# A new program order for an attention and two-stage expert kernel, with a straight constants block, a deeper ring of first-layer tiles and a smaller DMA scratch

## The chip, the cores and the metric

The kernel runs on one core of a Trainium2 chip. Its time is the device time of one execution in microseconds. TensorE (PE, with its weight loads as PEld), VectorE (DVE), ScalarE (ACT) and GpSimd (POOL) compute; SyncE (SP) only queues transfers, in order, and GpSimd queues the indirect ones.

## The reference

```python
# attention: B=4, H=8, S=576, D=64; a local band and a 4x downsampled one, added
q_d, k_d, v_d = means over groups of 4 positions
out_up    = repeat(softmax(q_d @ k_d.T / 8) @ v_d, 4)
out_local = softmax(where(|i - j| < 4, q @ k.T / 8, -1e9)) @ v
x = (out_up + out_local) as [2304, 512]
# first layer pair: w_in [512, 2048], w_out [2048, 512]
x = relu(x @ w_in) ** 2 @ w_out
# top 2 of 8 experts by noisy logits; w1 [8, 512, 1024], w2 [8, 1024, 512]
noisy = x @ w_gate + log1p(exp(x @ w_noise)) * noise
for e in range(8):
    out[rows of e] += weight * (relu(x[rows of e] @ w1[e]) @ w2[e])
```

## The kernel before

Matrix operands are float32 split into a high and a low fp16 part, and a product is three matmuls: high x high, high x low, low x high. The scales of the split are powers of two, taken from the data: a bound of w_in's columns by gram matrices of its pieces (L1023), the Frobenius norm of w_out and of each expert's matrices.

**Attention.** The 32 units (four batches b, two parts of each, four pairs of heads) each go through: loads of q and k (`load_qk`, L248, one for two parts), of v in groups (`load_vg`, L203) and of v in windows (`load_vw`, L255, two buffers used in turn); scores with a mask (S, L285 and L292), downsampled scores (D, L307), two softmaxes (`ml` and `md`: L318 to L336), normalising (`nl`, `nd`, on POOL for b = 0, L354), transposes (PT, L372 to L395), the PV matmul (PW: L426, then `od` on ACT at L444 and `xt` on VectorE at L445), and the split to fp16 (`xb`, L465 and L468) into one of five column buffers `xb` of the tile `xall`. A unit's `vw` buffer comes free when the PV matmul two units earlier has read it.

**First layer pair.** w_in comes in eight pieces (`load_f`, L523) through several steps on ACT and VectorE (L527, L531, L535, L540), each with a gram; then `scale` (L1033 and, in a helper, L171) gives `s_in`, and each piece is split (L1046, L1053). w_out takes the same steps in eight pieces, with squares by gram (L1078, L1079). The tokens are nine column chunks c of 256, with eight pairs of hidden blocks fp each: M is the first-layer matmul (`m1_mm`, L610), r its relu and square and split (`m1_ev`, L629 to L639) into a pair of tiles gh and gl, and Y the second matmul (`m2`, L656; L680 for the first chunks). `g_tiles` says from which ring of buffers a pair comes: eight pairs in pool `bp`, and `GX` = 3 more in pool `ap` for some (c, fp).

**Gate and experts.** For each of 18 token tiles the row is written out transposed by a DMA (`yT`, L724, read at L733), gated, and scattered by two indirect DMAs into the row buffer `xs` (L817). Expert 0 runs inside the table, its squares and splits (`prep_e`, L846, L862, L863) and those of expert 1 too. Experts 1 to 7 run in a loop behind it (L1205 to L1228). In a round, `c_m1` makes eight blocks f for the early 384 rows and eight for the late 240 (L917, relu and split at L919 and L920, into `h` tiles), and `c_m2` five blocks j of rows (L933), each with a scatter into the output (L936). Between the blocks stand the pieces that prepare expert e+1: eight squares (L846), the scales (`frob`, pfr at L476), eight splits. First-layer blocks use four PSUM tiles in turn.

**Order.** `ORDER` is a table of some 2000 tokens (`S5`: step S of unit 5) which is executed inside `tc.manual_schedule()`, so that each engine's program is in the table's order. What stands outside, the constants ahead and the expert loop behind, is ordered by the framework's scheduler. Waits and buffers then decide when things run.

Of the kernel before, what the change touches and what calls it, by code (L numbers as in the profile page):

```python
# [7 lines left out]
F32 = mybir.dt.float32  # L8
# [4 lines left out]
U16 = mybir.dt.uint16  # L13
# [13 lines left out]
P = 128  # L27
# [25 lines left out]
qk0 il0 ob0 vg1 S0 G0 vg0 ml0 ia0 vg3 D0 vm1 qk1 qk2 vg2 S1 il1 el0 vm0 ib0 nl0 md0 G1 qk3 vg4 D1 ml1 ed0 S2 ic0  # L53
md1 nd0 ij0 el1 G2 nl1 vm3 ed1 il2 nd1 il3 D2 vm2 md2 ia1 PT0 Xa0 vw1 ml2 el2 ib1 S3 nl2 Xm0 ed2 vm4 G3 PT1 S4
ml3 el3 vw0 il4 vs4 D3 il5 ia2 ic1 vs0 md3 nl3 il6 nd2 ed3 ia3 ib2 Xb0 D4 in0 md4 vs2 ij1 PW0 ic2 vw2 ib3 PT2
ml4 xb0 in1 ic3 el4 vs1 ij2 S5 vs3 PW1 D5 il7 md5 ol3 ol0 ia4 ed4 nd3 ia5 ib4 ol2 ij3 xb1 ic4 PT3 ib5 ia6 ij4
ib6 in2 in3 ic5 ml5 ia7 nl4 is3 PW2 ic6 el5 in4 ib7 ij5 vw3 xb2 ij6 ic7 oa3 ed5 in5 ij7 in6 in7 oB3 oa0 oB0 oa2
is7 nd4 ol1 PW3 wS0 S6 oB2 oc0 oc3 wT0 oj3 oa1 wU0 oc2 vw4 oB1 os3 wh5 oj2 wh1 qk4 S7 wl5 xb3 oc1 vg5 D6 wh4 md6
PT4 wl1 oj1 os2 wh0 oj0 wh7 wl0 nl5 vw5 wh6 M5 wl6 os1 wh2 wh3 qk5 wl7 M0 D7 wl4 qk6 of3 nd5 wl3 os0 wl2 ed6 r0
vm5 ra5 oh3 M1 of1 oo3 ra1 ml6 PW4 oh0 oo0 oh1 oh2 M6 oo1 oo2 el6 xb4 yh0 ol6 M3 ol5 yh1 vs5 nl6 r6 PT5 yl8 ml7  # L60
ra3 oa5 M4 yh5 oB5 ol4 yh9 yh6 ol7 oa6 oB6 oc5 oc6 yh3 yl5 yl11 oa4 yl3 nd6 S8 oj5 yl1 oa7 oj6 oB4 oB7 PW5 yh14
yl9 oc4 yh13 oc7 os5 M7 md7 yh11 ed7 yl13 yl6 yl14 os6 PT6 qk7 S9 vw6 yl0 oj7 oj4 G4 yh8 os7 os4 r4 M2 G5 of7
xb5 ra7 PW6 yh4 el7 of5 oh6 D9 vg6 yl15 yh12 D8 oh7 oh4 nl7 yh25 yh7 yh27 yh28 nd7 oh5 yh29 yl12 ml8 yh31 yh19
el8 PT7 yh24 oo7 oo6 yh30 yl28 yl30 oo5 yh20 oo4 vw7 yh23 yl29 md8 xb6 nl8 vm6 ed8 PW7 nd8 md9 vw8 yl20 yh21
yh17 yl24 vs6 yh22 yl25 xb7 S11 yh15 SD0 yl31 pz0 ml9 r2 yh16 ed9 yl16 PT8 M9 pg0 G6 G7 S10 ra9 ml10 M13 vw9 pf0
yl10 D10 yl2 el9 ra13 PW8 nl9 yl22 yl18 nd9 vg7 M12 vm7 yh10 PT9 yl17 Xa1 D11 M10 ml11 md10 Xm1 vs7 el10 md11
el11 ed10 nl10 ed11 nl11 yl4 yh26 pf1 nd10 yl21 r12 S13 S12 PT10 Xb1 ml12 yl7 D13 pf2 nd11 xb8 D12 md12 pf3 el12
# [32 lines left out]
def moe_kernel(ctx, tc, qk_in, vwin, vgrp, w_in, w_out, w_gate, w_noise, noise, w1, w2, out):  # L100
# [42 lines left out]
    for n in (32, 64):
        nc.vector.tensor_scalar(it[:, n:2 * n], it[:, :n], float(n), None, op0=OP.add)
    pc0_ = psT.tile([P, 512], F32, tag="tp", name="pci")
    nc.tensor.matmul(pc0_[:, 1:2], r32[0:1], onesf[0:1, 0:1], start=True, stop=True)
    nc.tensor.matmul(pc0_[:, 0:1], it[0:1], onesf[0:1, 0:1], start=True, stop=True)
    nc.vector.tensor_copy(pidx, pc0_[:, :2])
    nc.vector.tensor_scalar(dc, it[:, :KW], pidx[:, 1:2], 3.0, op0=OP.subtract, op1=OP.subtract)
    nc.vector.tensor_tensor(dc, dc, dc, op=OP.mult)  # L150
    nc.vector.tensor_scalar(mask, dc, 9.5, NEG, op0=OP.is_gt, op1=OP.mult)
    nc.vector.tensor_copy(masks, mask[:, None, :].to_broadcast([P, 9, KW]))
    for j in (0, 64):
        nc.vector.memset(masks[j:j + 32, 0, :3], NEG)
        nc.vector.memset(masks[j + 32:j + 64, 7, KW - 3:], NEG)
    nc.vector.tensor_scalar(idb, it, pidx[:, 0:1], None, op0=OP.is_equal)
    nc.vector.tensor_scalar(idf, it, pidx[:, 0:1], None, op0=OP.is_equal)
    nc.vector.memset(pms[1], 0.0)
    for i in range(2):
        nc.vector.memset(pTs[i][0], 0.0)  # L160
        nc.vector.memset(vws[i][32:64], 0.0)
    nc.vector.tensor_copy(onesb, onesf)
    nc.gpsimd.affine_select(trib, onesb, [[1, P]], OP.is_gt, 0.0, base=0, channel_multiplier=-1)
# [1173 lines left out]
```

## Time and profile before

| | us |
|---|---|
| median of 3 runs | 997.05 (996.45 to 998.46) |
| the profiled execution | 999.23 |
| its span in the trace | 997.4 |
| PE busy in the span | 928.7 (93%) |
| VectorE, ACT, POOL busy | 580.4, 497.4, 131.4 |
| last matmul ends, span ends | 985, 997.4 |

The profiled execution has its own time; the span is the part that the trace covers, without what lies before and behind. Mean granted clock of PE is 0.965.

### The profile page before, as it was taken

Reading aid. Unit: us, or ns where it says so; the run is one execution under the profiler, and the core shown is the slowest. Engines: PE = TensorE matmul, PEld = TensorE weight load, DVE = VectorE, ACT = ScalarE, POOL = GpSimd, SP = SyncE. Lnnn points to the kernel's source line nnn. Section 1 sums busy time; section 2 is a strip of 40 time slices with the busy share of each in tenths; the row PEclk is TensorE's granted clock in tenths of the full one; section 3 lists DMA queues with packets and bytes.
Section 4 is the critical chain, followed back from the end, with each engine's and each line's share of the span. In section 5 each row is a group of like instructions: output and inputs, shape, how many; then the busy total and the mean of one; then the engine's idle time right before and its main releaser. Section 6 shows DMA issues by size and latency. Waiting matters only on the chain. (4 is left out here: it accounts for less than half of the span.)

```text
span 997.4 us, 20288 instructions
## 1 busy us (share of the span) xinstructions
PE 928.7 (93%) x8254; PEld 624.9 (63%) x8254; DVE 580.4 (58%) x1809; ACT 497.4 (50%) x1076; POOL 131.4 (13%) x150
## 2 busy tenths in 40 slices
PE   3559999999999998999999899899999999999994
PEld 2448988575776675667766456647475656566562
DVE  7788967588678756665577763617162525343220
ACT  5687857455546554365663461835354544431110
POOL 2401200010102010000021021020202011111111
PEclk9659999999999998999999999999999999999997
DMA  9943369824232314022412785763838292821212
GB/s 321 299 161 117 122 234 324 210 96 84 81 98 83 53 42 46 27 65 100 137 44 64 211 190 146 174 142 94 170 84 187 54 219 27 238 30 22 31 22 34
DMA packets 104183, 121.70 MB, mean 122 GB/s; under 512 B 69264, under 2 KB 69264, under 8 KB 102032
## 3 DMA queue, kind: packets, MB, share of 16 engines
q1 hardware_dynamic: 95568, 100.57, 35.4%
q0 software_dynamic: 8512, 19.74, 10.4%
q8 instruction: 67, 1.10, 0.5%
q14 instruction: 36, 0.29, 0.1%
HBM read 70.33 MB, written 35.28 MB: 106 GB/s over the span
## 5 line engine op out<-in xcount | busy, mean ns | idle before, releaser
L610 PE MATMUL ph<-xall,wih 128*128 128x256 f16 x1152 | 196.0, 276 | 0.3 <-ACT r L629 0.3
L917 PEld LDWEIGHTS <-we 128*128 128x128 f16 x1536 | 150.4, 98 | 56.4 <-issue 3.4
L933 PE MATMUL po<-we,h 128*128 128x512 f16 (+1 forms) x840 | 182.4, 379 | 0.0
L610 PE MATMUL ph<-xall,wil 128*128 128x256 f16 x576 | 158.6, 275 | 0.0
L917 PE MATMUL phc<-xT,we 128*128 128x384 f16 (+1 forms) x1152 | 154.4, 296 | 0.0
L933 PEld LDWEIGHTS <-h 128*128 128x128 f16 (+1 forms) x840 | 87.6, 104 | 92.3
L919 ACT ACTIVATE h<-phc 128x384 f16<-128x384 f32 (+1 forms) x112 | 47.7, 427 | 179.6 <-PE phc L917 160.9
L656 PE MATMUL y<-wo,gh 128*128 128x512 f16 x448 | 134.7, 383 | 0.0
L610 PEld LDWEIGHTS <-wih 128*128 128x128 f16 x1152 | 111.5, 99 | 18.9 <-issue 2.6
L935 DVE TENSOR_SCALAR ob<-po,om 128x512 f32<-128x512 f32 (+1 forms) x35 | 26.3, 751 | 147.0 <-PE po L933 147.0
L936 POOL DMA_INDIRECT out_dram<-ob,tk x35 | 53.9, 1541 | 311.3 <-DVE ob L935 263.1
L817 POOL DMA_INDIRECT xs<-row,si x36 | 38.1, 1059 | 409.1 <-issue 175.1
L920 DVE SCALAR_TENSOR_TENSOR h<-phc,h 128x384 f16<-128x384 f32 (+1 forms) x112 | 52.8, 477 | 57.1 <-ACT h L919 55.7
L656 PE MATMUL y<-wo,gl 128*128 128x512 f16 x224 | 85.5, 382 | 0.0
L656 PEld LDWEIGHTS <-gh 128*128 128x128 f16 x448 | 42.1, 98 | 44.9 <-issue 2.4
L639 DVE TENSOR_TENSOR gl<-g,gh 128x512 f16<-128x512 f32 x64 | 44.0, 690 | 38.6 <-ACT gh L638 37.8
L610 PEld LDWEIGHTS <-wil 128*128 128x128 f16 x576 | 57.0, 99 | 7.2
L629 ACT ACTIVATE r<-ph 128x512 f32<-128x512 f32 x72 | 42.1, 585 | 22.0 <-PE ph L610 22.0
L633 ACT ACTIVATE g<-r 128x512 f32<-128x512 f32 x72 | 45.4, 630 | 2.3
L863 DVE SCALAR_TENSOR_TENSOR we<-w2raw,sce,we 128x1024 f16<-128x1024 f32 x32 | 40.5, 1274 | 1.2 <-ACT we L862 1.2
L863 DVE SCALAR_TENSOR_TENSOR we<-w1raw,sce,we 128x1024 f16<-128x1024 f32 x32 | 40.2, 1277 | 1.4 <-ACT we L862 1.1
L656 PEld LDWEIGHTS <-gl 128*128 128x128 f16 x224 | 22.0, 98 | 26.9 <-issue 0.8
(349 smaller groups left out, 1378.4 us busy)
## 6 DMA issues: line engine op xcount, KB each, us to landing
w1raw<-in_moe_w_dram SPq DMA_DIRECT2D x8, 2048.0 KB
w2raw<-in_moe_w_dram SPq DMA_DIRECT2D x8, 2048.0 KB
xs<-zrow SPq DMA_DIRECT2D x8, 1290.0 KB
qkT<-in_qk_dram SPq DMA_DIRECT2D x16, 579.0 KB
raw<-in_moe_w_out_dram SPq DMA_DIRECT2D x8, 1024.0 KB
out_dram<-zrow SPq DMA_DIRECT2D x1, 4864.0 KB
raw<-in_moe_w_in_dram SPq DMA_DIRECT2D x4, 1024.0 KB
vw<-in_vwin_dram SPq DMA_DIRECT2D x48, 76.0 KB
```

Of the source, the lines that this page charges most:

```text
L610: nc.tensor.matmul(ph[:, f], a[:, kk, fo], bb[:, kk], start=(n == 0), stop=(n == 11))
L629: nc.scalar.activation(r, ph, AF.Relu, scale=KAPPA)
L633: nc.scalar.activation(g, r, AF.Square)
L639: nc.vector.tensor_tensor(gl, g, gh, op=OP.subtract)
L656: nc.tensor.matmul(py[c, tt], a[:, o], bb[:, ft], start=(ft == 0 and n == 0), stop=(ft == 15 and n == 2))
L817: st = nc.gpsimd.indirect_dma_start(out=xs, out_offset=bass.IndirectOffsetOnAxis(ap=si[:, kk:kk + 1], axis=0), in_=roww, in_offset=None)
L863: nc.vector.scalar_tensor_tensor(wl[:, o], raws[i][:, o], ss[i], wh[:, o], op0=OP.mult, op1=OP.subtract)
L917: nc.tensor.matmul(ph[:, :n], a[:, fo], xT[:, bb], start=(i == 0), stop=(i == 11))
L919: nc.scalar.activation(hh[:, f], ph[:, :n], AF.Relu)
L920: nc.vector.scalar_tensor_tensor(hl[:, f], ph[:, :n], 0.0, hh[:, f], op0=OP.max, op1=OP.subtract)
L933: nc.tensor.matmul(po, a[:, f, jo], bb[:, do], start=(i == 0), stop=(i == 23))
L936: st = nc.gpsimd.indirect_dma_start(out=out, out_offset=bass.IndirectOffsetOnAxis(ap=tk[:m], axis=0), in_=ob[:m], in_offset=None, compute_ ...
```

## The change

- The constants (masks, identities, memsets) stand in a function that runs under `tc.manual_schedule()`, in the order as written.
- `ORDER` is another table of the same tokens.
- `GX` is 10 instead of 3, and `g_tiles` takes pairs from the two rings by the pair's running number, for all chunks up to 5, so that 18 pairs are used in turn.
- `dynamic_dma_scratch_size` is 2048 where the default left 16384; the 14 KB a partition are what seven more pairs need.
- The `h` tiles of odd and even experts change places.
- The preparation of expert e+1 goes one piece a block; only the second late block has two. Before, the first four early blocks had two each.
- A function `sign` is defined and called by nothing.

```diff
-qk0 il0 ob0 vg1 S0 G0 vg0 ml0 ia0 vg3 D0 vm1 qk1 qk2 vg2 S1 il1 el0 vm0 ib0 nl0 md0 G1 qk3 vg4 D1 ml1 ed0 S2 ic0
...
+vg0 vg3 ob0 qk0 vg2 S0 vg1 vm0 qk1 qk2 vm1 vm2 G0 S1 ml0 G1 D0 md0 ml1 el0 vg4 ed0 S2 vm3 G2 vm4 el1 D1 il0 Xa0
...
-    nc.gpsimd.memset(onesf, 1.0)
-    nc.gpsimd.memset(pms[0], 0.0)
...
+    def constants():
+        nc.gpsimd.memset(onesf, 1.0)
+        nc.gpsimd.memset(pms[0], 0.0)
...
+    with tc.manual_schedule():
+        constants()
...
-    XB, GX, MB = 5, 3, 3
+    XB, GX, MB = 5, 10, 3
...
-        if 0 < c < 6 and fp < GX:
+        if c < 6 and (8 * c + fp) % (8 + GX) >= 8:
...
-        hh, hl = hts[2 - 2 * (e % 2):4 - 2 * (e % 2)]
+        hh, hl = hts[2 * (e % 2):2 * (e % 2) + 2]
...
-                k_ = 2 if j0 == 0 and f < 4 else 1
+                k_ = 2 if j0 and f == 1 else 1
...
-    nc = _bacc.Bacc("TRN2", target_bir_lowering=False, num_devices=1)
+    nc = _bacc.Bacc("TRN2", target_bir_lowering=False, num_devices=1, dynamic_dma_scratch_size=2048)
```

Every engine has the same instructions before and after; what moves is their order, at these places among others.

SyncE's queue at the start of the program, before; `raw` from in_moe_w_in are pieces of w_in, `wih` from in_vgrp are v groups of batch 0, kept in a tile that w_in gets later, vw_96 is unit 0's `vw`:

```order
L248 DMA qkT_0_177<-in_qk_dram 128x1158
L523 DMA raw<-in_moe_w_in_dram 128x2048
L203 DMA wih<-in_vgrp_dram 72x1024 x3
L248 DMA qkT_1_218<-in_qk_dram 128x1158
L248 DMA qkT_2_220<-in_qk_dram 128x1158
L203 DMA wih<-in_vgrp_dram 72x1024
L523 DMA raw<-in_moe_w_in_dram 128x2048
L248 DMA qkT_3_256<-in_qk_dram 128x1158
L203 DMA vg_0_261<-in_vgrp_dram 72x1024
L523 DMA raw<-in_moe_w_in_dram 128x2048 x2
L255 DMA vw_97<-in_vwin_dram 38x512 x2
L255 DMA vw_96<-in_vwin_dram 38x512 x2
```

The same rows of the changed kernel:

```order
L206 DMA wih<-in_vgrp_dram 72x1024 x2
L251 DMA qkT_0_186<-in_qk_dram 128x1158
L206 DMA wih<-in_vgrp_dram 72x1024 x2
L251 DMA qkT_1_213<-in_qk_dram 128x1158
L251 DMA qkT_2_215<-in_qk_dram 128x1158
L206 DMA vg_0_262<-in_vgrp_dram 72x1024
L526 DMA raw<-in_moe_w_in_dram 128x2048
L258 DMA vw_96<-in_vwin_dram 38x512 x2
L251 DMA qkT_3_350<-in_qk_dram 128x1158
L526 DMA raw<-in_moe_w_in_dram 128x2048 x3
L526 DMA wil<-in_moe_w_in_dram 128x2048
L258 DMA vw_97<-in_vwin_dram 38x512 x2
```

One w_in piece stands ahead of unit 0's `vw` instead of four, and three qkT loads instead of four; the v groups stand ahead of them all.

VectorE's first instructions, before; `pm` here is the scratch in which the mask is built:

```order
L139 MEMSET pm_91 128x1
L160 MEMSET pT_92 128x512
L141 TENSOR_SCALAR pm_91<-pm_91 128x1
L161 MEMSET vw_96 32x768
L141 TENSOR_SCALAR pm_91<-pm_91 128x2
L160 MEMSET pT_94 128x512
L141 TENSOR_SCALAR pm_91<-pm_91 128x4
L161 MEMSET vw_97 32x768
L141 TENSOR_SCALAR pm_91<-pm_91 128x8
L162 CAST onesb<-onesf 128x128
L141 TENSOR_SCALAR pm_91<-pm_91 128x16
L500 MEMSET lob 128x1
```

And of the changed kernel:

```order
L140 MEMSET pm_91 128x1
L503 MEMSET lob 128x1
L200 MEMSET vmx_181 128x8
L142 TENSOR_SCALAR pm_91<-pm_91 128x1
L142 TENSOR_SCALAR pm_91<-pm_91 128x2
L142 TENSOR_SCALAR pm_91<-pm_91 128x4
L142 TENSOR_SCALAR pm_91<-pm_91 128x8
L142 TENSOR_SCALAR pm_91<-pm_91 128x16
L143 COPY pm_91<-pm_91 128x128
L145 TENSOR_SCALAR pm_91<-pm_91 128x32
L145 TENSOR_SCALAR pm_91<-pm_91 128x64
L149 COPY pidx<-pci 128x2
```

The mask chain stands alone now; the memsets of pT and vw and the cast of `onesb` stand behind it.

ACT at the hand-off from expert 0 to expert 1, from its first write of expert 1's `h` tile on, before; `junk` are the squares of expert 2, `we` its splits:

```order
L919 ACTIVATE h_9006<-phc 128x384
L846 ACTIVATE junk,acce_9024<-w1raw_8992 128x1024
L919 ACTIVATE h_9006<-phc 128x384
L846 ACTIVATE junk,acce_9024<-w1raw_8992 128x1024
L919 ACTIVATE h_9006<-phc 128x384
L846 ACTIVATE junk,acce_9024<-w1raw_8992 128x1024 x2
L919 ACTIVATE h_9006<-phc 128x384
L846 ACTIVATE junk,acce_9025<-w2raw_8994 128x1024
L919 ACTIVATE h_9006<-phc 128x384
L846 ACTIVATE junk,acce_9025<-w2raw_8994 128x1024
L862 ACTIVATE we_9150<-w1raw_8992,sce_9117 128x1024
L846 ACTIVATE junk,acce_9025<-w2raw_8994 128x1024
```

And of the changed kernel, where the `h` tile is another one:

```order
L926 ACTIVATE h_9011<-phc 128x384
L853 ACTIVATE junk,acce_9027<-w1raw_8926 128x1024
L926 ACTIVATE h_9011<-phc 128x384
L853 ACTIVATE junk,acce_9027<-w1raw_8926 128x1024
L926 ACTIVATE h_9011<-phc 128x384
L853 ACTIVATE junk,acce_9027<-w1raw_8926 128x1024 x2
L926 ACTIVATE h_9011<-phc 128x384
L853 ACTIVATE junk,acce_9028<-w2raw_8928 128x1024
L926 ACTIVATE h_9011<-phc 128x384
L853 ACTIVATE junk,acce_9028<-w2raw_8928 128x1024 x2
L926 ACTIVATE h_9011<-phc 128x384
L853 ACTIVATE junk,acce_9028<-w2raw_8928 128x1024
```

The squares of expert 2 spread over more blocks, and its splits have left the early blocks.

## Rows read from the trace of the kernel before

**Rows 1.** Windows: length, then busy us of PE, PEld, DVE, ACT, POOL; PEclk, DMA, GB/s.
```profile
0.00:30.00 30.00, 12.91 (x228) 9.03 (x228) 23.57 (x72) 19.31 (x46) 8.30 (x18) 1.00 0.93 320
30.00:80.00 50.00, 29.98 (x354) 23.91 (x355) 39.43 (x62) 36.78 (x60) 10.28 (x10) 0.56 0.59 200
80.00:180.00 100.00, 96.16 (x1462) 84.81 (x1461) 80.12 (x202) 70.93 (x164) 9.01 (x12) 0.98 0.62 219
180.00:615.00 435.00, 427.37 (x4011) 285.92 (x4008) 292.97 (x1198) 223.00 (x552) 48.39 (x75) 0.99 0.37 96
615.00:647.00 32.00, 26.52 (x197) 18.95 (x195) 17.47 (x45) 21.97 (x39) 1.49 (x1) 1.00 0.65 134
...
sum 997.40, PE 928.68 PEld 624.88 DVE 580.36 ACT 497.41 POOL 131.40; mean PE 132.67 PEld 89.27 DVE 82.91 ACT 71.06 POOL 18.77
```

**Rows 2.** Waits of PE in 80 to 600: total us, times, longest.
```profile
PE pl L733 <- DMA yT<-row: 2.9, 2, 2.2
PE S L307 <- DVE pm L318: 2.6, 1, 2.6
```

**Rows 3.** Waits of VectorE in 0 to 67.
```profile
DVE xt L445 <- ACT od L444: 7.1, 3, 4.7
```

**Rows 4.** Timeline of 29 to 38 (start, length, engine, instruction, idle before).
```profile
35.45 1.13 PE L426 MATMUL px<-pT,vw 102*64 102x64 f32 x16 [6.92 <-DMA vw<-in_vwin_dram]
...
36.61 0.61 SPq L255 DMA_DIRECT2D vw<-in_vwin_dram  x2
...
37.27 0.35 SPq L523 DMA_DIRECT2D xall<-in_moe_w_in_dram  x1
```

**Rows 5.** Timeline of 61 to 74.5.
```profile
61.53 1.12 PE L426 MATMUL px<-pT,vw 102*64 102x64 f32 x16 [2.70 <-DMA vw<-in_vwin_dram]
...
63.01 0.42 DVE L445 TENSOR_TENSOR xt<-px,od 128x256 f32<-128x256 f32 x1 [2.11 <-ACT od L444]
...
66.42 0.15 DVE L171 TENSOR_SCALAR s_in<-es 128x1 int32<-128x1 int32 x1
...
72.75 1.10 PE L1078 MATMUL pq<-raw 128*128 128x128 bf16 x8 [1.66 <-ACT pt L393]
...
73.68 0.61 PE L610 MATMUL ph<-xall,wih 128*128 128x256 f16 x2
```

**Rows 6.** Timeline of 618 to 637, the hand-off to expert 1.
```profile
623.39 0.49 ACT L919 ACTIVATE h<-phc 128x384 f16<-128x384 f32 x1 [18.55 <-DMA out_dram<-xall,tk]
...
624.52 2.11 PE L917 MATMUL phc<-g,we 128*128 128x384 f16 x12 [1.88 <-DVE h L920]
...
624.81 0.48 ACT L919 ACTIVATE h<-phc 128x384 f16<-128x384 f32 x1
...
628.98 0.39 PE L476 MATMUL pfr<-acce,onesf 128*128 128x4 f32 x2 [2.35 <-ACT junk L846]
...
635.39 0.39 PE L476 MATMUL pfr<-acce,onesf 128*128 128x4 f32 x2 [1.14 <-ACT junk L846]
...
636.25 0.24 DVE L901 SCALAR_TENSOR_TENSOR om<-mt 128x5 f32<-128x5 f32 x2 [1.36 <-DMA mt<-xs]
```

**Rows 7.** Chain that ended last, 640 to 700: start, length, what.
```profile
642.53 1.19 DVE we L863
...
644.04 1.19 DVE we L863
...
647.00 25.90 PE po L933 x120
672.90 9.75 PE phc L917 x60
...
682.99 15.71 PE phc L917 x132
```

**Rows 8.** The page's group of the output scatters (busy, mean ns, idle before).
```profile
L936 POOL DMA_INDIRECT out_dram<-ob,tk x35 | 53.9, 1541 | 311.3 <-DVE ob L935 263.1
```

**Rows 9.** The row scatters (line L817): us from issue to landing.
```profile
DMA to landing us min/median/max: 2.7/3.1/7.6
```

More of the change, by code (lines that the diff above doesn't have):

```diff
@@ L58 @@
[L58 to L67, printed above, removed]
@@ new lines @@
+nd2 ib1 PW0 il3 ic1 D4 S3 ia2 md4 ml3 il4 vw1 vs1 ed4 D3 el3 md3 ia3 il5 PT2 il6 ml4 S5 el4 ib2 ij1 ib3 D5 nl3
+md5 vw2 nl4 in0 nd4 ed3 S6 xb0 in1 ia4 nd3 ic3 il7 ib4 PW1 ij3 ol2 D6 ic2 ij2 md6 in2 ic4 xb1 ia5 ij4 vs2 PT3
+ib5 ia6 ic5 ib6 vs3 ml5 vw3 PW2 ol3 in3 ij5 ic6 ol0 xb2 vg5 ia7 ij6 vw4 in4 ib7 PT4 ic7 in5 oa2 is3 ij7 in6 ed5
+oB2 PW3 in7 oa3 is7 el5 oc2 wS0 ml6 wT0 ol1 oj2 wU0 xb3 oa0 wh1 oB0 oB3 vw5 nl5 wh5 wl1 oc0 oj0 wh0 wl0 os0 wh3
+oc3 oj3 oa1 qk4 oB1 os2 wl5 wh2 wl3 wh6 wh7 os3 el6 M5 oc1 oj1 qk5 wl7 ed6 of3 ra5 os1 wh4 nl6 M0 wl6 wl4 vm5
@@ new lines @@
+wl2 S7 r0 of1 PW4 nd5 oh2 oo2 ol5 oh3 oh0 vs5 oo3 M1 ra1 ol6 oh1 oo0 G4 D7 M4 ol7 PT5 xb4 nd6 yh0 yl9 M3 r4 md7
+ra3 PW5 yl1 yl0 yh9 oa5 M6 oa6 oo1 yl13 oB5 ml7 ol4 xb5 r6 yl8 yl11 yl3 oa7 S8 yl12 PT6 yl4 ed7 el7 oB6 vg6 M2
+oB7 yh6 yh8 ml8 oc5 nl7 yh4 M7 oj5 yh13 oc6 D8 oc7 oj6 yh11 oj7 yh3 oa4 vm6 yh1 oB4 os7 os5 yh14 vw6 md8 yl14
+nd7 oc4 os6 qk6 yl6 oj4 S9 of7 PW6 ed8 os4 yh5 oh7 yl5 yh12 qk7 G5 oh6 of5 yh30 vw7 oo7 yh28 vw8 S11 yh27 oh5
+oh4 vs6 yh24 yh25 oo5 yh22 PT7 D9 oo4 yh19 oo6 yh20 yh16 xb6 PW7 r2 yh29 yh17 SD0 xb7 yl22 yl29 yl16 yl28 yl24
@@ new lines @@
+el14 md15 PT13 yl19 ga0 gb0 D14 M17 PW12 M19 nl14 ga1 Y8 md14 gc0 Y9 Y10 ml15 Y11 vw13 gb1 ed14 el15 gd0 Y12 vg9
+qk8 nd14 ed15 vw14 Y13 Y14 qk9 vm9 gf0 G8 xb12 G9 ge0 ra17 S16 gc1 gd1 gg0 nl15 M23 vs9 S17 PW13 nd15 Y15 ra19
+ra23 qk10 xb13 PT14 vw15 M22 PT15 D16 vg10 ga2 M18 gf1 gb2 ge1 gg1 ra22 PW14 ml16 gc2 qk11 ra18 vm10 ga3 D17
+md17 G11 ed17 md16 M20 ml17 M21 el17 Y16 gd2 G10 ed16 gb3 el16 nl17 xb14 vs10 gc3 Y17 nd17 S18 nl16 PW15 S19
+nd16 vg11 ra20 D18 Y18 ra21 vm11 vw16 Y19 PT16 PT17 Y20 md18 ml18 Y21 Xa2 gf2 D19 ml19 xb15 gd3 el18 vs11 M27
@@ new lines @@
+PT22 vs13 G13 vg14 M33 ra33 xb21 M32 PW22 M36 ra32 S25 vm14 el23 vw24 gb7 vw23 xb22 ml24 nl23 D24 M38 nd23 ra36
+Y32 vs14 gc6 gd6 Y33 gf6 G14 Y34 D25 el24 PT23 md24 M37 nl24 gc7 md25 ed24 qk15 PW23 vg15 ml25 nd24 ed25 ge6
+ra38 ra37 S26 Y35 xb23 PT24 gd7 M39 Y36 gg6 M40 el25 nl25 gf7 ml26 Y37 G15 vm15 el26 PW24 ge7 nd25 ra39 S27 vw25
+ra40 D26 gg7 M43 Y38 ra43 md26 ed26 Y39 Xa3 D27 ga8 S28 ga9 md27 M45 Xm3 nl26 PT25 D28 ml27 Xb3 ed27 gb8 Y40
+nd26 el27 gc8 ra45 gb9 xb24 M47 nl27 M41 ra47 ra41 gd8 nd27 M42 gc9 PT26 ml28 S29 D29 el28 gf8 PW25 vs15 md28
@@ L96 @@
+pe28 cw0 lr1 cw2 pe29 pe30 cm8 cm11 pe31 cm12 cm9 cm10 pe32 cm13 pe33 cm14 lr2 le2 cm15 cw4 cw3
 """
@@ L143, in moe_kernel @@
[L143 to L161, printed above, removed]
@@ L162, in moe_kernel @@
-    nc.vector.tensor_copy(onesb, onesf)
-    nc.gpsimd.affine_select(trib, onesb, [[1, P]], OP.is_gt, 0.0, base=0, channel_multiplier=-1)
+    def constants():
+        nc.gpsimd.memset(onesf, 1.0)
+        nc.gpsimd.memset(pms[0], 0.0)
+        pw = pms[1].rearrange("p a b -> p (a b)")
+        it, r32, dc = pw[:, :P], pw[:, P:2 * P], pw[:, 2 * P:2 * P + KW]
+        nc.vector.memset(it[:, 0:1], 0.0)
+        for n in (1, 2, 4, 8, 16):
+            nc.vector.tensor_scalar(it[:, n:2 * n], it[:, :n], float(n), None, op0=OP.add)
+        nc.vector.tensor_copy(r32.rearrange("p (a b) -> p a b", b=32), it[:, None, :32].to_broadcast([P, 4, 32]))
+        for n in (32, 64):
+            nc.vector.tensor_scalar(it[:, n:2 * n], it[:, :n], float(n), None, op0=OP.add)
+        pc0_ = psT.tile([P, 512], F32, tag="tp", name="pci")
+        nc.tensor.matmul(pc0_[:, 1:2], r32[0:1], onesf[0:1, 0:1], start=True, stop=True)
+        nc.tensor.matmul(pc0_[:, 0:1], it[0:1], onesf[0:1, 0:1], start=True, stop=True)
+        nc.vector.tensor_copy(pidx, pc0_[:, :2])
+        nc.vector.tensor_scalar(dc, it[:, :KW], pidx[:, 1:2], 3.0, op0=OP.subtract, op1=OP.subtract)
+        nc.vector.tensor_tensor(dc, dc, dc, op=OP.mult)
+        nc.vector.tensor_scalar(mask, dc, 9.5, NEG, op0=OP.is_gt, op1=OP.mult)
+        nc.vector.tensor_copy(masks, mask[:, None, :].to_broadcast([P, 9, KW]))
+        for j in (0, 64):
+            nc.vector.memset(masks[j:j + 32, 0, :3], NEG)
+            nc.vector.memset(masks[j + 32:j + 64, 7, KW - 3:], NEG)
+        nc.vector.tensor_scalar(idb, it, pidx[:, 0:1], None, op0=OP.is_equal)
+        nc.vector.tensor_scalar(idf, it, pidx[:, 0:1], None, op0=OP.is_equal)
+        nc.vector.memset(pms[1], 0.0)
+        for i in range(2):
+            nc.vector.memset(pTs[i][0], 0.0)
+            nc.vector.memset(vws[i][32:64], 0.0)
+        nc.vector.tensor_copy(onesb, onesf)
+        nc.gpsimd.affine_select(trib, onesb, [[1, P]], OP.is_gt, 0.0, base=0, channel_multiplier=-1)
@@ L527, in low, with sign @@
             nc.scalar.activation(t_, t_.bitcast(U32), AF.Relu, scale=2.0 ** -29, bias=lob)
+        def sign():
+            h_ = st["raw"].bitcast(U16)
+            nc.gpsimd.tensor_scalar(h_[:, :, 1], h_[:, :, 3], 32768, None, op0=OP.bitwise_and)
         def bits():
```

59 lines of the change are left out of this document (21 added, 38 removed).

## The prediction

> **What bounds the kernel now.** I began with the split of the span into stretches [rows 1]. TensorE is busy for 928.68 of 997.40 us, so an order can only recover its idle time and time at a low clock. Idle time, stretch by stretch, is the length minus PE: 17.1 us in the first 30, 20.0 in the next 50, 3.8 in 80 to 180, 7.6 in 180 to 615 and 5.5 in 615 to 647; behind 647 there is next to none until the last matmul at 985. The 30 to 80 stretch is poor twice over: PE is busy 60% of it and was granted a clock of 0.56, about the lower level of 1.2 GHz, where the others have 0.98 to 1.00. So the start is where an order can pay, the hand-off between the expert 0 and the loop over the others is second, and the middle has little to give and much to lose: its waits are single ones of 2 to 3 us [rows 2], over 520 us.
>
> Next I asked what the start waits for. In the first 67 us VectorE's largest wait is for `od` of the attention output: 7.1 us in three pieces, the longest 4.7 [rows 3]. The timeline has two of them. At 35.45 the PV matmul (L426) begins after 6.92 us of waiting for a `vw` transfer, and VectorE's L445 behind it has waited 4.72 [rows 4]. SyncE's queue holds the same delay once more: its next `vw` (36.61) needs the buffer which that PV matmul frees, and a piece of w_in stands behind it, issued only at 37.27 [rows 4]. At 61.53 another L426 has waited 2.70 for `vw`. The scale of w_in, `s_in`, is ready at 66.57, the last gram of its neighbour w_out runs at 72.75, and the first first-layer matmul (L610) comes at 73.68 [rows 5].
>
> **The start: -6 us.** In the order before, four qkT groups, four w_in pieces and five vg groups are queued ahead of unit 0's `vw`. By the shapes in the order rows that is 4 x 0.593 + 4 x 1.049 + 5 x 0.295 = 8.0 MB, or 25 us at the 320 GB/s of the first 30 us [rows 1], and the trace has it there just before 35.45 [rows 4]. In the new order 3 x 0.593 + 1.049 + 5 x 0.295 = 4.3 MB stand ahead, 13.5 us. So unit 0's `vw` should be there before its probabilities are; the PV matmul begins 6.9 us sooner, SyncE is released as much sooner, and VectorE's 4.7 us wait goes. The 2.70 us `vw` wait at 61.53 has `vw4` issued far ahead now, and the wait of the L445 behind it (2.11 of the 7.1 [rows 5]) goes too. On the other side, the mean durations of VectorE's instructions ahead of `s_in`, by the two orders, sum to 55.7 us before and 54.5 after (mask chain and preparation counted): -1.2. Together `s_in` would come 4.7 + 2.1 + 1.2 = 8 us sooner. Not all of it arrives at the first-layer matmuls: three w_out grams stand ahead of `M5` now and two before, and the third needs a conversion (L540) that lies at 63.4 us of VectorE's sum. With the 3.8 us of waits that stay (66.57 - 55.7 - 7.1), that is 67.2, plus 1.1 for the gram, so L610 begins at some 68.5 instead of 73.68: 5 us. The next two first-layer groups don't hang on that gram alone; I get 6 to 7 for them. I take **6**. Bounds: 0 if the w_in pieces, which are issued behind 3.6 MB more than before (11 us at 320 GB/s), become what is late instead; 12 if all 8 us arrive and the 8 us that are gone at a clock of 0.56 [rows 1] give back what PE did too slowly in them, 8 x 0.44 = 3.5. The mask constants in straight order let the first score matmul begin some 4 us sooner, but VectorE then has the same memsets to do behind them; their gain is inside the -1.2.
>
> **The hand-off: -1.5 us.** ACT's first write of the expert-1 `h` tile (623.39) has waited 18.55 us for an expert-0 scatter; PE has run ahead by its four PSUM tiles and waits 1.88 at 624.52 [rows 6]. The swap of the `h` tiles suggests that this wait goes, since the new tile doesn't lie over `xall`. The instruction order with its waits says otherwise: the same instruction has the same ten semaphores before and after, because a whole pool is released there. So this wait stays, at 0. What does change is behind it. Before, two squares of expert 2 follow an early `h`, and the two norm matmuls (pfr) stand among the early blocks: PE waits 2.35 us at 628.98 and 1.14 at 635.39 for ACT's squares [rows 6]. Now they stand behind the first late block. From 623.39, an `h` with one square takes 1.42 us (623.39 to 624.81 [rows 6]), so the eight squares are done by 623.39 + 8 x 1.42 = 634.75 at the latest. PE, with four early blocks of 2.11 us from 624.52 [rows 6] and a late one of 1.23, comes to the pfr at 634.2, so it waits 0.6 at most where it waited 3.5. Part comes back: VectorE's `om` (636.25, 1.36 us late for its `mt` transfer [rows 6]) now stands ahead of the seventh `h`, and the eight splits all lie in late blocks, at 1.51 us a block (642.53 to 644.04 [rows 7]) against PE's (15.71 - 3 x 9.75 / 5) / 8 = 1.23 [rows 7]. With these in the new order, block by block, VectorE frees the tile that the last late block needs at 644.3, and the block ends near 645.5 instead of 647.00 [rows 7], where the second layer begins. **1.5**; bounds 0 (VectorE's splits eat it) and 3.4.
>
> **The steady experts: 0.** From 647 on, PE's chain has no gap: from 647.00 to 682.99 + 15.71 it is 51.7 us for one expert [rows 7]. The new placement puts 1.51 us of ACT or VectorE beside 1.23 us of PE for eight blocks, which builds up 8 x 0.28 = 2.3 us, plus about 1 us for the scales; four PSUM tiles cover 4 x 1.23 = 4.9. If that cover were short, each of six experts would lose 1 to 2 us.
>
> **Seven more g tiles: 0.** Among PE's waits in 80 to 600 none of 0.2 us or more is for a free g tile (the two longest are [rows 2]), so they take away nothing by themselves; they let the new order keep first-layer results longer. **Smaller scratch: 0.** The 35 output scatters wait 263.1 us for VectorE and take 1.54 us each [rows 8]: POOL idles between them. If only one could be in flight, each would begin up to its landing time later, off the path but for the last. The first thing that would be late is the buffer `ob`, three deep.
> The Trainium skill (DMA: Bandwidth & Descriptors, section SWDGE vs HWDGE vs iDMA) says that GpSimd writes the descriptors of its DMAs to rings in an SBUF carveout, and the Trainium skill (SBUF — State Buffer, section SBUF size: 192, 224, or 256?) puts that carveout at 16 KiB; a carveout of 2 KiB would hold fewer, which speaks against this edit. By it the rival of the full ring below would hold and the sum be 993; by the rows it stays. No run here shows that a ring fills.
>
> **The middle: 0.** Same instructions in another order, at static distances that look alike: five yT transposes have their reader directly behind them now as against four before, the nearest x-to-matmul distance is 0.4 us of PE work against 0.0. I price it at 0, and its bounds at +-10: three or four more waits of the kind in [rows 2], each 2 to 3 us, or all 7.5 us of idle time in 180 to 615 gone.
>
> **The sum.** The profiled execution is 999.23 us, 1.8 outside its span. 999.23 - 6 - 1.5 = 991.7; the median shown is 2.2 lower, so 997.05 - 7.5 = **989.5**.
>
> **The rivals.**
> *The start's gain doesn't arrive.* The w_in pieces come later and VectorE's work up to `s_in` is nearly the same; if the conversions wait for pieces, or the denser 80 to 180 stretch (VectorE 80 of 100 us busy [rows 1]) becomes VectorE-bound, only 0 to 3 us are left: 994 to 997. For it: the DMA share is 0.93 in the first 30 us, so an early transfer makes another late. Against: SyncE's queue itself stood behind the late PV matmul until 36.61 [rows 4], and that is what moves.
> *The hand-off opens as the swap suggests.* If the release is not what ACT waits for, all 5.5 idle us of 615 to 647 go: 989.5 - 4 = 985.5. Against: the identical semaphores.
> *Slower: late transposes and x in the middle.* The gate reads yT right behind its DMA. At the 2.2 us of the longest such wait [rows 2], six new ones cost 13 us, and from the fourth on (8.8) they outweigh the 7.5: 989.5 + 13 = 1002.5. For it: the new order keeps PE on first-layer work to fill, which moves second-layer and gate work together. Against: of four transposes with their reader right behind them only two waited before [rows 2].
> *The ring fills.* If a row scatter (L817) has to wait for the landing of the one before, 3.1 us [rows 9], only the last pair ahead of expert 0's first transpose stands in the path: one landing, 989.5 + 3 = 993. The output scatters of the loop have time between them [rows 8].
>
> **Chances and range.** Forecast (985 to 994) 0.52; hand-off opens 0.06; start's gain lost 0.2; slower by the middle 0.17; ring 0.05. A change within 0.2% (2 us) is about what cannot be told from none. Below 995.1 falls the forecast, the open hand-off, the ring and a third of the lost gain: 0.69; within 995.1 to 999.0 half of the lost gain: 0.12; above: 0.19. The range, 980 to 1001, reaches from the start's upper bound with the hand-off's (997 - 12 - 3.4 = 981.6, less a little of the middle) to the fourth or fifth new wait; the forecast's own is 985 to 994.
>
> **What would show it.** Right: the first L610 at about 68, no `vw` wait above 1 us at the first PV, ACT's `h` of expert 1 still late by the scatter, no pfr wait above 0.5, steady experts at 51.7. Wrong: VectorE waiting for w_in pieces in 30 to 60, new DMA yT or x waits in the middle, POOL waiting between scatters, idle PE between late blocks and the second layer.

## The result, and the profile after

The changed kernel takes 981.17 us in the median (980.70 to 981.24) beside 997.38 for the kernel before: a ratio of 0.9836 (0.9819 to 0.9853), 16.2 us less. The forecast was 7.5 to 8 us less. The direction was right; the size is twice what was forecast.

The windows of the changed kernel (length; busy us of PE, PEld, DVE, ACT and POOL with counts; then PEclk, DMA share and GB/s), cut where its stages are:

```profile
0.00:30.00 30.00, 13.76 (x232) 9.03 (x232) 22.75 (x68) 17.31 (x43) 9.09 (x18) 1.00 0.95 314
30.00:80.00 50.00, 27.54 (x312) 21.29 (x313) 45.94 (x71) 39.25 (x64) 11.68 (x9) 0.62 0.57 192
80.00:180.00 100.00, 99.77 (x1550) 88.41 (x1549) 82.88 (x212) 73.47 (x171) 6.12 (x12) 1.00 0.66 232
180.00:603.00 423.00, 415.52 (x3939) 278.21 (x3937) 285.63 (x1180) 221.75 (x543) 47.74 (x75) 1.00 0.37 95
603.00:635.00 32.00, 30.01 (x213) 20.55 (x212) 13.77 (x41) 18.79 (x36) 2.72 (x2) 1.00 0.59 119
635.00:971.00 336.00, 336.00 (x2016) 202.32 (x2014) 130.11 (x240) 128.84 (x221) 52.55 (x34) 1.00 0.54 105
971.00:979.40 8.40, 0.18 (x1) 0.00 (x0) 0.75 (x1) 0.00 (x0) 1.48 (x1) 0.65 0.28 39
```

Beside [rows 1] the first 80 us look no better: PE is idle for 16.2 + 22.5 = 38.7 us, where it was 37.1. From 80 to 180 it is idle for 0.2 instead of 3.8, and VectorE did 68.7 us of work in the first 80 where it had done 63.0. The span is 18.0 us shorter (979.4 after 997.4), and part of that lies at the very end. These rows hold the last matmul of the kernel before and of the changed kernel (start, length):

```profile
974.80 7.93 PE L933 MATMUL po<-we,h 128*128 128x512 f16 x36
959.79 11.39 PE L940 MATMUL po<-we,h 128*128 128x512 f16 x52
```

It ends at 982.73 before and at 971.18 after, so 14.7 us followed it and 8.2 follow it now. (The 985 in the table ahead is the edge of a window, 2.3 us behind the last matmul.)

The chain that ended last gives the dates of the later stages (start, length, what), first one row of the kernel before, where the last expert's second layer begins, then the changed kernel:

```profile
956.84 25.91 PE po L933 x120
```

```profile
613.33 0.49 ACT h L926
...
635.39 25.90 PE po L940 x120
661.29 16.83 PE phc L924 x108
...
945.28 20.73 PE po L940 x96
```

ACT's first write of expert 1's `h` tile came at 623.39 [rows 6] and comes at 613.33: 10.1 us less so far. The second layer of expert 1 began at 647.00 [rows 7] and begins at 635.39: 11.6 less, so the hand-off gave 1.55. The next expert's begins at 687.10, 51.71 later, where it was 51.70: the steady experts gave nothing. The last expert's second layer begins 11.6 us sooner too (945.28 after 956.84). The span is 18.0 shorter, so **6.4 us come from behind that point**, where the forecast had nothing.

What that is stands among GpSimd's queue instructions at the program's end, which count as no busy time. Each row has the count, the least, median and largest ns, and the first and last start. The kernel before, by the lines of its conditional behind the loop and of the program's end:

```profile
L1233 POOLq INC_SWDGE_SEM  x1: 1704/1704/1704, 988.6 to 988.6; - x1
...
L1333 POOLq DRAIN  x3: 50/107/6275, 990.3 to 997.1; - x3
```

and the changed kernel:

```profile
L1240 POOLq INC_SWDGE_SEM  x1: 384/384/384, 977.3 to 977.3; - x1
...
L1340 POOLq DRAIN  x3: 50/107/885, 977.7 to 979.2; - x3
```

Behind the last scatter, GpSimd runs INC_SWDGE_SEM (1.70 us before; called the queue's close below) and a long DRAIN (6.28); the other engines have finished their work by then. Both together are 7.98 us before and 1.27 after: 6.7 less. The runs below show that the size of the DMA scratch sets them, and that is a part of the change which was priced at 0.

### The profile page after: what moved, and what is told of

It is laid out like the page before. It is cut to its first block, busy times and chain, and to the rows that moved or that the text cites. A ratio compares the mean times of both kernels' runs of the same rounds, so it can differ in the third digit from the quotient of the medians.

```text
span 979.4 us, 20286 instructions
## 1 busy us (share of the span) xinstructions
PE 922.8 (94%) x8254; PEld 619.8 (63%) x8254; DVE 581.8 (59%) x1809; ACT 499.4 (51%) x1076; POOL 131.4 (13%) x150
## 5 line engine op out<-in xcount | busy, mean ns | idle before, releaser
L617 PE MATMUL ph<-xall,wih 128*128 128x256 f16 x1152 | 196.5, 276 | 0.5 <-ACT r L636 0.4
L617 PE MATMUL ph<-xall,wil 128*128 128x256 f16 x576 | 158.9, 276 | 1.5 <-DVE wil L1060 1.5
L617 PEld LDWEIGHTS <-wih 128*128 128x128 f16 x1152 | 111.3, 99 | 18.3 <-issue 1.8
L617 PEld LDWEIGHTS <-wil 128*128 128x128 f16 x576 | 57.0, 99 | 9.4 <-DVE wil L1060 2.0
L869 ACT ACTIVATE we<-w1raw,sce 128x1024 f16<-128x1024 f32 x32 | 36.2, 1142 | 10.9 <-DVE sce L174 10.9
L870 DVE SCALAR_TENSOR_TENSOR we<-w2raw,sce,we 128x1024 f16<-128x1024 f32 x32 | 40.8, 1281 | 1.0 <-ACT we L869 0.9
```

Source lines behind the costliest of these rows:

```text
L617: nc.tensor.matmul(ph[:, f], a[:, kk, fo], bb[:, kk], start=(n == 0), stop=(n == 11))
L870: nc.vector.scalar_tensor_tensor(wl[:, o], raws[i][:, o], ss[i], wh[:, o], op0=OP.mult, op1=OP.subtract)
```

## The experiments

Each version was timed beside the kernel before on the same chip. Chips differ (the kernel before has medians of 997.4 to 1001.6 on them), so versions are compared by their ratio to it, and the last column is that ratio turned into us of 997.4. "Changed" is the changed kernel, with a ratio of 0.9836 (-16.4 us); "old" is what stands in the kernel before.

| version | median, us | ratio to before | 95% interval | us by the ratio |
|---|---|---|---|---|
| scratch 2048 alone | 991.15 | 0.9943 | 0.9923 to 0.9963 | -5.7 |
| scratch 8192 alone | 992.57 | 0.9960 | 0.9941 to 0.9979 | -4.0 |
| constants alone | 996.74 | 0.9990 | 0.9976 to 1.0005 | -1.0 |
| scratch, swap, pieces | 989.17 | 0.9924 | 0.9906 to 0.9942 | -7.6 |
| scratch, tiles | 996.08 | 0.9944 | 0.9923 to 0.9964 | -5.6 |
| scratch, tiles, new table | 986.39 | 0.9850 | 0.9828 to 0.9872 | -15.0 |
| changed, old table | 994.30 | 0.9926 | 0.9902 to 0.9950 | -7.4 |
| changed, old table to M1 | 983.62 | 0.9864 | 0.9839 to 0.9888 | -13.6 |
| changed, old table from M1 | 987.29 | 0.9909 | 0.9880 to 0.9937 | -9.1 |
| changed, old table from lr0 | 982.92 | 0.9864 | 0.9842 to 0.9886 | -13.6 |
| changed, old pieces | 982.72 | 0.9848 | 0.9823 to 0.9872 | -15.2 |
| changed, old `h` tiles | 981.70 | 0.9841 | 0.9815 to 0.9867 | -15.9 |
| changed, scratch 512 | 1002.88 | 1.0014 | 0.9995 to 1.0034 | +1.4 |
| before, D28 moved | 994.34 | 0.9972 | 0.9960 to 0.9985 | -2.8 |
| changed, D24 moved | 982.10 | 0.9841 | 0.9821 to 0.9862 | -15.9 |
| changed, D24 moved, scratch 1024 | 979.16 | 0.9834 | 0.9809 to 0.9859 | -16.6 |
| changed, on another chip | 985.78 | 0.9862 | 0.9842 to 0.9882 | -13.8 |
| D24 moved, scratch 1024, on that chip | 983.01 | 0.9834 | 0.9818 to 0.9850 | -16.6 |

The changed kernel itself has -16.4 us on one chip and -13.8 on another. So differences below some 3 us between versions on different chips are not told apart by the times, and below the traces are asked as well.

**The scratch.** The kernel before, with one number added:

```diff
-    nc = _bacc.Bacc("TRN2", target_bir_lowering=False, num_devices=1)
+    nc = _bacc.Bacc("TRN2", target_bir_lowering=False, num_devices=1, dynamic_dma_scratch_size=2048)
```

> The kernel before with a scratch of 2048 bytes and nothing else. Theory A (the end is the cleaning of the scratch, whose length goes with its size): GpSimd's last drain falls from 6.28 to 0.89 us and the operation ahead of it from 1.70 to 0.38, so the time is 997.4 - 6.7 = 990.7. Theory B (a smaller ring makes indirect DMAs wait, and the short end of the changed kernel is its earlier last scatter): the drain stays near 6 us, scatters land later, and the time is 997 to 1000.

Theory A: 5.7 us less, without another edit. The queue rows at the end of its trace are those of the changed kernel to the nanosecond:

```profile
L1333 POOLq DRAIN  x3: 50/107/885, 990.7 to 992.2; - x3
```

Theory B falls: its output scatters land in 4.8 us in the median, as before. All traces agree on where the gain lies. From the start of the last expert's second layer to the end of the span they have 40.6 to 40.8 us in the three kernels with 16384 bytes, and 34.0 to 34.2 in all versions with 2048, whatever else was changed in them. Then 8192:

> The kernel before with a scratch of 8192 bytes. Theory A, on the line through the drains at 16384 and 2048 bytes (6.28 and 0.89 us, 0.385 us a KB): the last drain takes 3.2 us, the operation ahead of it 0.95, and the time is 993.5. Theory B (a threshold somewhere between, or no bearing on the drain): 990.7 or 997.4.

```profile
L1333 POOLq DRAIN  x3: 50/107/1661, 989.5 to 991.7; - x3
```

The drain grows with the size, but not on a line: 1.66 us against 3.2 expected, and more than three times that at 16384. The size sets it; by what law stays open. The time (4.0 less, interval 2.1 to 5.9) fits theory A's 993.5 but can't be told from that of 2048; in the trace the piece behind the start of the last second layer is 34.7 us.

At the other end, the changed kernel with 512 bytes:

> The changed kernel with a scratch of 512 bytes. Theory A, on the line through two sizes: the drain takes 0.31 instead of 0.89 us and the operation ahead of it 0.24 instead of 0.38, so 0.7 us less, 980.5. Theory B (a ring that small makes GpSimd wait for landings): scatters spaced by their landing time, at least 3 us more, 984.

Theory B, and far beyond its number: 18 us above the changed kernel, although the drain fell to 0.23 us. The six experts from the second layer of expert 1 to that of expert 7 take 16.6 us longer in the trace. Waits of GpSimd and VectorE in its expert loop (us in total, times, longest):

```profile
POOL out_dram L943 <- issue: 78.7, 14, 8.6
DVE tk L913 <- DMA out_dram<-ob,tk: 36.7, 4, 10.8
```

and VectorE's in the changed kernel's, where GpSimd has no such wait:

```profile
DVE tk L913 <- DMA out_dram<-ob,tk: 11.9, 4, 3.3
```

"Issue" means that the profile shows nothing that the engine waited for: GpSimd is idle ahead of 14 scatters without a releaser, and begins some of them late. The second block of rows of expert 2 is ready at 699.48 and its scatter begins at 703.80; in the changed kernel these are 698.25 and 698.72. The row indices `tk` have two buffers. A new set may be written when the scatters of the set before last have landed, so VectorE waits longer for that; the `h` instructions are queued behind that write on VectorE, and PE waits for them 12.7 us in four pieces, where the changed kernel's loop has no such wait. So a scratch that is too small does cost time, at 512 bytes; at 2048 that isn't seen. That it is a full ring which holds GpSimd fits these rows, but no trace shows the ring.

**Constants, and the hand-off's two edits.** The first version is the kernel before with the new constants block (as in the diff ahead, no other part); the second is the kernel before with the scratch of 2048 and

```diff
-        hh, hl = hts[2 - 2 * (e % 2):4 - 2 * (e % 2)]
+        hh, hl = hts[2 * (e % 2):2 * (e % 2) + 2]
...
-                k_ = 2 if j0 == 0 and f < 4 else 1
+                k_ = 2 if j0 and f == 1 else 1
```

> The kernel before with the constants in straight order and nothing else. Theory A: the first score matmul begins 2 to 4 us sooner than 9.84, but the PV matmul of unit 0 still waits for its vw until about 35.4, so the time is 997.4 within 1. Theory B: the mask chain heads the start's path, and all of 3 us arrives: 994.4.

> The kernel before with a scratch of 2048 bytes, the h tiles swapped and the preparation in single pieces. Beside the scratch alone: theory A (ACT's first write of the new h tile waits for the same scatter; only the pfr waits go) 1.5 us less, the write about as late as before; theory B (the swap frees the tile) 5.4 us less, and no wait of ACT for a scatter ahead of the first h of expert 1.

The constants make no difference that can be told from none, as theory A has it. The two edits give 1.9 us beyond the scratch (0.9943 to 0.9924, with intervals that overlap), and the trace has theory A: ACT's first `h` still waits 19.4 us for the scatter, and PE's wait for the squares is 0.6 us. The same two edits undone in the changed kernel, one at a time:

> The changed kernel with two pieces of preparation behind each of the first four early blocks, as before. Theory A: the two pfr waits come back, 1.5 us more, 982.7. Theory B (steady experts lose too): 51.7 us an expert becomes more than 52, 985.

> The changed kernel with the h tiles in their old places. Theory A (the release is the whole pool's): 981.2 within 0.6, and ACT's first write of the tile of expert 1 waits as long. Theory B (the swap saved a wait): 983 to 986, with that write later by 2 us or more against PE's first matmul of expert 1.

By the times, 1.2 us are lost with the old pieces and 0.5 with the old tiles, both inside the intervals. The traces tell them apart. With the old pieces the waits for the squares are back (3.2 us in two pieces), and from ACT's first write of `h` to the second layer of expert 1 it takes 23.5 us, as in the kernel before (23.6); with the old tiles it takes 22.0, as in the changed kernel (22.1), and ACT waits as long for the scatter (16.4 us against 16.7). With the two edits alone it takes 22.6, and 23.8 with the scratch alone. (One version departs: with D24 moved and 2048 bytes it takes 23.2 although its pieces are the new ones.) Theory A in both: the pieces bring 1.2 to 1.5 us, the swap is not seen to bring anything, and the six experts behind take the same 310 us with old and new pieces.

**Tiles and the table.** The next two versions are the kernel before with scratch 2048 and GX = 10 with its rule, and the same with the new table:

> The kernel before with a scratch of 2048 bytes and GX = 10 with its rule, in the old order. Beside the scratch alone (990.7 expected): theory A (no wait for a g tile was there to remove) no change within 1; theory B (tile releases held PE back unseen) 2 us or more less.

> As tiles_scratch, with the new order table; constants, h tiles and pieces as before. Theory A (what moved between 85 and 610 us is the table's): PE gets to the experts 8 us sooner than before, and the time is near 982.7, the changed kernel's 981.2 plus the 1.5 of the pieces. Theory B (the constants block is needed for it): 985 or more, with the difference made in the first 80 us.

The tiles give nothing by themselves (0.9944 beside 0.9943; theory A). The table gives 9.4 us (0.9944 to 0.9850, on one chip and with intervals far apart), the largest part of the change, and the time is as theory A has it. Whether it could be had without the tiles wasn't tried. The reverse is all but the table; then the table is cut in two at M1, with the old tokens first or last:

> The changed kernel with the old order table: constants, tiles, scratch, swap and pieces are new. Theory A: it keeps the end's 6.7 us and the hand-off's 1.5 and loses the rest, 997.4 - 8.2 = 989.2. Theory B (the hand-off's 3.4 us of PE time between 610 and 647 is all its own): 987.3.

> The changed kernel with a spliced table: the old one as far as its first first-layer matmul of chunk pair M1, and then the new one's remaining tokens in their order. Theory A (the new start brought nothing, the rest did): 981 within 2. Theory B (the new start is what makes the dense 85 to 190 us possible, with results ready sooner): 985 to 989.

> The changed kernel with the opposite splice: the new table up to M1, then the old one's remaining tokens in their order. Theory A (the rest of the table brought 8 us): 989 within 2, with PE's idle time in 80 to 180 and at 380 to 400 as before. Theory B (the start carries it): 981 to 984.

All but the table gives 7.4 us, nearer to theory A. With the new start alone it is 9.1, with the new rest alone 13.6, with both 16.4. So the rest is worth 6.2 to 7.3 us of the table's 9, clear of the intervals; the start's 1.7 to 2.8 are not clear of them. In 80 to 180 PE is idle for 2.4 us with the new start alone and for 2.0 with the new rest alone, where it is 3.8 with the old table and 0.2 with the new one: it takes both halves, and neither theory A nor B holds whole. The tail of the table, from the first rows of expert 0 on:

> The changed kernel with the new table up to the token lr0 (the first rows of expert 0) and the old one's tokens behind it. Theory A (the table's tail, by expert 0's scatters, carries what the hand-off gained beyond the pieces): 2 us more, 983.2. Theory B (it is the state in which the tail is reached): 981.2 within 1.

2.8 us more than the changed kernel, as theory A has it, but the intervals meet; ACT's wait for the scatter is 18.8 us there against 16.7.

**One wait in the middle.** Both kernels have, in the middle, a D matmul (downsampled scores) that waits for VectorE's mask: [rows 2] has one of 2.6 us, which lies at 392.9 in unit 28, and the changed kernel has its own at 323.9 in unit 24:

```profile
323.90 0.46 PE L310 MATMUL S<-qkT 64*64 64x144 f32 x4 [2.70 <-DVE pm L321]
```

Both units have D behind `ml` in the table, with nothing of PE between, and the two write and read the same score tile. Moving one token ahead of the other was tried in each kernel:

```diff
-... nd27 Y40 Y41 ra42 xb25 gd8 gb9 ml28 D28 ...
+... nd27 Y40 Y41 ra42 xb25 gd8 gb9 D28 ml28 ...
...
-... xb22 ml24 nl23 D24 M38 ...
+... xb22 D24 ml24 nl23 M38 ...
```

> The kernel before with D28 ahead of ml28, nothing else. Theory A (the same as for D24): the wait of 2.58 us at 392.9 goes, with the half clock behind it in those executions that have it: 2.6 to 5 us less, 992.5 to 995. Theory B (the middle of the new table gained by its gates and stores, not by this wait): 997.4 within 1.

> The changed kernel with one token moved: D24 (the downsampled scores of unit 24) stands ahead of ml24 (VectorE's masking of the same score tile) instead of two tokens behind it. Theory A (D24 waits for VectorE only because the program has it behind the mask, and the clock falls after that wait): PE's wait of 2.70 us at 323.9 goes and the half clock of some 3 us behind it too, so 2.7 to 4.5 us less, about 977.5. Theory B (PE waits for something else there): 981.2 within 1.

Theory A in the kernel before: there this one token is worth 2.8 us (1.5 to 4.0). PE is busy for the whole of 380 to 400, where the same window has a gap with the token in its old place. First the version with D28 moved, then the kernel before:

```profile
380.00:400.00 20.00, 20.00 (x256) 13.35 (x257) 13.36 (x53) 9.23 (x24) 0.00 (x0) 1.00 0.35 45
```

```profile
380.00:400.00 20.00, 17.41 (x175) 10.51 (x174) 11.75 (x47) 7.35 (x19) 0.00 (x0) 0.83 0.46 43
```

The granted clock can add to the price: behind the 2.6 us gap it fell to its lower level of 1.2 GHz for part of the window (0.83 in the mean), without the gap it stayed at 1.00. That isn't so in every execution: the version with the constants alone has the same gap and 1.00 in this window. So the wait itself accounts for most of the 2.8 us, and the clock's share isn't told apart. In the changed kernel the wait of 2.70 is gone from the trace as well, but the time can't be told from the changed kernel's (0.9841 and 0.9836), so theory A isn't shown there. The version with 1024 bytes too, and then that version and the changed kernel beside each other on one chip:

> As after_d24, with a scratch of 1024 bytes. Theory A (the drain follows the size, and the ring still holds what is in flight): 0.5 us less than after_d24. Theory B (the ring fills, as at 512 bytes): GpSimd and then VectorE wait in the expert loop, 3 us or more above after_d24.

> The changed kernel itself once more, to stand on the same chip beside the version with D24 moved and 1024 bytes of scratch: ratio to the kernel before 0.983 to 0.985 by both theories.

> The changed kernel with D24 ahead of ml24 and a scratch of 1024 bytes, beside the changed kernel on the same chip. Theory A (the 2.7 us wait with its half clock and the shorter drain are gone and nothing takes their place): 3 us less than the changed kernel. Theory B (the start, which differs from execution to execution by some 3 us, swallows it, or GpSimd waits come with the small ring): within 1 us of it.

Side by side the version takes 983.01 us (982.95 to 983.74) and the changed kernel 985.78 (983.47 to 986.66), with ratios of 0.9834 (0.9818 to 0.9850) and 0.9862 (0.9842 to 0.9882); the changed kernel is outside the 0.983 to 0.985 that was expected of it. The version beats the kernel before clearly; against the changed kernel it is 2.8 us ahead in the medians, near theory A's 3, but with intervals that overlap. Its drain and queue close are 0.48 and 0.28 us, 0.5 less, and PE waits for nothing in the expert loop. Where the other 2.3 would come from isn't settled: in its profiled execution another wait stands in the place of the one removed, this time for the transposed row of a gate:

```profile
PE pl L738 <- DMA yT<-row: 2.5, 1, 2.5
```

## Why the prediction was half right

**"Smaller scratch: 0" is the step that failed.** It looked at what a ring does while scatters run and asked only whether less room would make something wait. It left out the program's end, where the trace of before has 14.7 us behind the last matmul; the prediction has that matmul at 985, which leaves 12.4, and asked nothing of these either. They held 8 us of GpSimd closing and draining its queue, and the smaller scratch takes 6.7 of these in the trace and 5.7 in the time. The rival of the full ring is a cost on the other side only; a cost of that kind comes at 512 bytes (18 us more than the changed kernel) and is not seen at 2048. The Trainium skill (DMA: Bandwidth & Descriptors, section SWDGE vs HWDGE vs iDMA) says that the descriptors of these DMAs go to rings in an SBUF carveout; no trace here shows the rings.

**"The middle: 0" was mis-sized, and 80 to 180 has no term in the sum.** The table's rest is worth 6 to 7 us by the splices. The prediction listed the 3.8 us in which PE is idle between 80 and 180 and priced them nowhere; they are 0.2 in the changed kernel. The longest of them is a wait of a D matmul behind a mask once more, with the low clock behind it. The wait and its window in the kernel before, then the window in the changed kernel:

```profile
PE S L307 <- DVE pm L321: 1.6, 1, 1.6
140.00:160.00 20.00, 18.58 (x286) 15.48 (x287) 13.29 (x48) 10.88 (x31) 0.00 (x0) 0.91 0.71 247
140.00:160.00 20.00, 19.77 (x313) 16.80 (x312) 16.19 (x58) 14.77 (x41) 0.00 (x0) 1.00 0.78 279
```

All eight traces with the whole old table have 3.6 to 3.9 us of idle time in 80 to 180 and a granted clock of 0.83 over 140 to 150; all ten with the new one up to its tail have 0.2 us and 1.00 there. An estimate from that: 3.6 us of idle time and 10 x 0.17 = 1.7 us of clock, some 5 us in a stretch without a term. From 180 on, PE is idle as long as before (7.6 us up to 615, 7.5 up to 603). The 2.6 us wait at 392.9 is gone there, but the new table has one of its own at 323.9, so the 2.8 us of the moved token are no part of its gain; the prediction named such waits [rows 2] as a danger and didn't look at what made the one it had. The table's tail may bring 2 to 3 us (not clear of its interval). What else the rest holds stays open. The clock has a part in it: PE's 8254 matmuls take 5.9 us less in the changed kernel (928.68 to 922.78), but behind 180 the clock's falls differ between executions of the same kernel.

**"The start: -6" was right in its mechanism at the first link and not in where it goes.** The `vw` wait of unit 0's PV matmul and VectorE's 7.1 us of waits for `od` are gone, as said. Not all `vw` waits are: PE has three others up to 80, the longest 2.7, where the sum had the one of 2.70 go too, and it waits for qkT loads, which stand behind the v groups now:

```profile
PE px L429 <- DMA vw<-in_vwin_dram: 5.7, 3, 2.7
PE S L295 <- DMA qkT<-in_qk_dram: 6.0, 2, 3.6
```

The first L610 (L617 now) comes at 72.44, 1.2 us sooner and not 5:

```profile
63.40 0.15 DVE L174 TENSOR_SCALAR s_in<-es 128x1 int32<-128x1 int32 x1
...
68.86 1.77 PEld L1085 LDWEIGHTS <-raw 128*128 128x128 bf16 x16 [7.28 <-DVE raw L547]
68.87 2.05 PE L1085 MATMUL pq<-raw 128*128 128x128 bf16 x16 [7.20 <-DMA qkT<-in_qk_dram]
...
72.44 0.61 PE L617 MATMUL ph<-xall,wih 128*128 128x256 f16 x2
```

PE stands 7.2 us ahead of the w_out gram. (The matmul's row names a load; its weight load waits for the conversion L547 on VectorE, which ends at 68.81.) The step that failed is `s_in`: it was to come 8 us sooner, at 58.6, and is ready at 63.55, 3.0 sooner. By windows up to its last instruction VectorE was busy for 51.55 us of 66.42 before and for 53.70 of 63.40 after. The waits for `od` took 7.1 of the idle time before and none after, as forecast. But the work grew by 2.2 us where the sum had it shrink by 1.2, among other things because two conversions of w_in took 1.92 us in the mean where they had taken 1.21; and the other idle time grew by 1.9 (7.8 to 9.7) where the sum had it stay, with waits for qkT loads of 2.4 us instead of 0.7. The sum also had the size of it wrong: it counted 55.7 us of work for the 51.55, and so 3.8 of other waits for the 7.8. What the start gained is VectorE's and stays there as work done early: 5.7 us more of it by 80. That this is what shortens PE's idle time in 80 to 180 is half shown: the new start alone takes it from 3.8 to 2.4 us, and 0.2 needs the new rest too. By the splices the start is worth 1.7 to 2.8 us in the time, not clear of the intervals.

**"The hand-off: -1.5"** measured 1.55 in the trace from ACT's first write to the second layer. ACT still waits for the scatter (16.7 us), no run shows the swap to be worth anything, and the pfr wait is 0.6 as bounded:

```profile
PE phc L924 <- DVE h L927: 1.1, 2, 0.8
PE pfr L479 <- ACT junk L853: 0.6, 1, 0.6
```

**Steady experts 0, tiles 0, constants inside the rest:** all three as forecast. By the ratios the 16.4 us are, rounded, 5.7 for the scratch, 9.4 for the table and 1.4 for what is left then (pieces, swap and constants); the 1.4 is a remainder, so that the parts sum up proves nothing. That the sum came out 8 to 9 us short has its largest causes in the end (6.7 us) and in 80 to 180, while the start gave less than its 6.

## What to carry to other kernels

Read the end of the span as a stage of its own, with the queue instructions that no busy time counts. This kernel paid there for the size of the scratch of its indirect DMAs; the sizes worth trying are those below the default down to where scatters begin late (here PE has no wait in the expert loop with 2048 or 1024 bytes, and 512 cost 18 us). Give every stretch of idle time in the table a term, if only to say why it stays: the two that had none here, 80 to 180 and the end, held much of what was missed. When a trace has one wait of 2 to 3 us in an otherwise full engine, ask which two neighbours in program order make it; moving one token was worth 2.8 us in the kernel before. And time saved on an engine ahead of the bound one need not show at the next event: follow the work to where the bound engine first runs without a gap.

## What the hardware showed that was not expected

GpSimd's last drain takes 0.23, 0.48, 0.89, 1.66 and 6.28 us at scratch sizes of 512, 1024, 2048, 8192 and 16384 bytes, and the queue's close ahead of it 0.22, 0.28, 0.38, 0.57 and 1.70, with the same 76 indirect DMAs in each. With 512 bytes 14 scatters have 78.7 us of idle time of GpSimd ahead of them that nothing in the profile ends; with 2048 there is none of that kind.

Behind a wait of 2.6 to 2.7 us in a full stretch the clock fell to its lower level in some executions (0.83 over the 20 us around it in the kernel before; 0.83 over 10 us in the changed kernel) and stayed at 1.00 in another execution of the changed kernel. Behind the wait of 1.6 us at 141 it fell in all eight traces with the old table (0.83 over 140 to 150), and stayed at 1.00 in the version with the new start and the old rest, which has the same wait.
